# A long-convolution and MLP kernel: the filter spectrum and its exchange in two channel halves, all spectral products on VectorE, the identity made on the chip, and a new order of the pieces

## The chip, the cores and the metric

The kernel runs on one core of one Trainium2 chip. The metric is the time of one execution on the device, in microseconds (us); lower is better. "Span" is what the profile of one execution covers, here about 2 us less than the time. Every ratio of two kernels in this text is the mean time of one kernel's fast runs over that of the other's fast runs of the same rounds on the same chip, with a 95% interval; it is therefore not quite the ratio of the medians that are quoted beside it.

Engines are called PE (TensorE matmul), PEld (its weight load), DVE (VectorE), ACT (ScalarE), POOL (GpSimd) and SP (the engine that issues most DMAs here). PEclk is the TensorE clock that was granted, as a share of full speed. In this kernel PE writes its results to a memory called PSUM, and DVE or ACT copies them from there to SBUF, where the other data on the chip lies; that copy is called an eviction.

## The reference

One block `A` is a causal long convolution by FFT with a gate; one block `B` is an MLP. Each follows a layernorm, and the pair is applied twice.

```python
def _A_ref(q, k, v, shift_k, ssm_k, ssm_D):          # S = 2048, D = 512
    k_shift = sum of 4 shifted copies of k, each times a column of shift_k   # (shortened)
    kv = k_shift * v
    y_f = rfft(pad(kv, 2S)) * rfft(pad(ssm_k, 2S))
    y = irfft(y_f)[:, :S]                            # in bfloat16
    return q * (y + kv * ssm_D)
def _B_ref(x, w1, b1, w2, b2):                       # F = 1376
    return gelu(layernorm(x) @ w1 + b1) @ w2 + b2

x = A_q
x = x + _A_ref(layernorm(x), A_k, A_v, A_shift_k, A_ssm_k, A_ssm_D)
x = x + _B_ref(layernorm(x), ...)
x = x + _A_ref(layernorm(x), ...)                    # the same k, v, filter: y is the same
x = x + _B_ref(layernorm(x), ...)
```

The convolution result does not depend on `x`, so the kernel computes it once. What follows it, eight passes of the MLP over 512 tokens, is the second part of the kernel.

## The kernel before

The transforms are matmuls against tables. The kernel is written as named pieces, each with one engine, and one list gives the order in which they are issued. An engine executes its own pieces in that order, so a piece that waits holds up all later ones on its engine.

How to read the list: `K2S0.P10` is the piece `K2S0` on PE with numbered buffers (PSUM buffer 1, another buffer 0); a name ending in `e` is the eviction of that piece from PSUM; `.A`, `.D`, `.G` and `.S` are ACT, DVE, POOL and the DMA queue. The pieces that matter here, with `c` for a 128-channel chunk (0 to 3):

- `lK`, `lk`, `lv`, `lW`, `lx`: loads. `KTc`: transposes of a loaded filter chunk. `dtc`: adds `ssm_D` to the filter's first time step. `dgc`: four diagonal 128x128 matrices for the shift, made of the identity.
- `KcS`, `KcT`, `K2j`: the stages of the filter's transform. `saj`, `sbj`: DMAs that copy the finished spectrum with its two partition halves exchanged (real against imaginary parts), a quarter at a time.
- `kvc`, `UcS`, `UcT`, `Xcj`: the shifted `k`, times `v`, and its transform. `Tcj`: the product of a piece of that spectrum with the filter's, 16 in all. `Vcj`, `TPc`, `Yc`: the inverse. 
- `s`, `ga`, `gl`, `gp`, `gb`, `h`, `hs`, `LT`: gate and layernorm of the first two MLP passes, and transposes. `ph`: the first matmul of the MLP, with gelu on ACT.

The list in its parts that matter (cut):

```python
ORDER = """
lK2.S dg0.D lK1.S lK3.S ... dg2.D lk3.S lk1.S dg3.D dg1.D dt2.D KT2.P0
...
K0T1.P1 lM.S kT1e.A K3T1.P2 K0T1e.D K27.P0 K24.P3 K3T1e.D K27e.A kv31.P1 K24e.D
K214.P2 kvm31.D K215.P0 K214e.A ... K29.P1 ... K212.P2 ... K28.P1 ... K21.P3 ... K23.P2 ...
... K213.P2 U0S3e.A K211.P3 K25.P1 ...
sb3.S sa3.S K22.P2 ... K20.P1 ... K210.P0 sa0.S sb0.S ... K26.P2
... sa2.S sb2.S U1S2e.D U2S3.P1 U2S0e.A sa1.S sb1.S ...
... X10.P10 ... T10.G0 ... T11.D1 ... T13.G2 ... T00.D0 ... T01.G1 ...
"""
```

The code of the pieces concerned (cut):

```python
nc.scalar.dma_start(sT[:], A_shift_k.rearrange("(ct p) k -> p ct k", p=P))
nc.scalar.dma_start(IDt[:], ident_h.ap().bitcast(BF16))      # the identity comes from HBM
...
dt = plan.add(f"dt{ct}", {"D": 70}, [lK[ct]], lambda it, ct=ct: nc.vector.tensor_tensor(
    Kraw[:, ct, 0:1], Kraw[:, ct, 0:1], Dc[:, ct:ct + 1], ALU.add))
...                                                          # KT waits for dt
for j in range(4):                                           # the exchange, by quarters of all channels
    r = slice(8 * j, 8 * j + 8)
    a = load(f"sa{j}", KSW[0:64, r, :], ZK[64:128, r, :], 2 ** 19, KW[4 * j:4 * j + 4] + ...)
    b = load(f"sb{j}", KSW[64:128, r, :], ZK[0:64, r, :], 2 ** 19, KW[4 * j:4 * j + 4] + ...)
...
def mul(it, px=px, k0=k0, c0=c0):                            # T: 128x2048 elements, by DVE or POOL
    eng = nc.vector if it["eng"] == "D" else nc.gpsimd
    ...
    eng.tensor_tensor(view(Tb[it["slot"]["T"]], [2, 8, CW]), x2, kk, ALU.mult)
```

Of the kernel before, what the change touches and what calls it, by code (L numbers as in the profile page):

```python
# [9 lines left out]
BF16 = mybir.dt.bfloat16  # L10
# [8 lines left out]
lK2.S dg0.D lK1.S lK3.S lH.S lv0.S lK0.S lk2.S lW.S lv1.S lG.S lk0.S dg2.D lk3.S lk1.S dg3.D dg1.D dt2.D KT2.P0  # L19
KT2e.D dt1.D K2S0.P10 KT1.P2 K2S0e.A K2S1.P3 dt3.D KT1e.D KT3.P0 K2S1e.A K2S3.P1 KT3e.D K1S0.P21 K2S3e.A K2S2.P3  # L20
K1S0e.D K1S1.P0 K2S2e.A K1S2.P1 K1S1e.D K1S3.P2 K1S2e.A K2T0.P3 K1S3e.A K3S0.P12 K2T1.P0 dt0.D K3S0e.D K2T0e.A
KT0.P2 K2T1e.D kT2.P1 KT0e.A K3S2.P3 kT2e.D K1T0.P0 K3S2e.A K3S1.P2 K1T0e.D K3S3.P1 K3S1e.A K0S0.P30 K1T1.P0
K0S0e.D K3S3e.A K0S2.P2 K1T1e.D K0S1.P1 K0S2e.A K3T0.P3 K0S1e.A K0S3.P0 kT0.P2 K0S3e.D K3T0e.A kT3.P1 K0T0.P0
kT3e.D kT0e.A kT1.P3 K0T0e.D K0T1.P1 lM.S kT1e.A K3T1.P2 K0T1e.D K27.P0 K24.P3 K3T1e.D K27e.A kv31.P1 K24e.D
K214.P2 kvm31.D K215.P0 K214e.A kv00.P3 K215e.D K29.P1 kvm00.D K212.P2 K29e.A kv10.P0 K212e.D U0S0.P31 kvm10.D
K28.P1 U0S0e.A kv01.P2 K28e.D U1S0.P00 kvm01.D K21.P3 U1S0e.A U1S1.P1 K21e.D K23.P2 U1S1e.A U0S2.P0 K23e.D
U0S1.P3 U0S2e.A kv20.P1 U0S1e.D U0S3.P0 kvm20.D K213.P2 U0S3e.A K211.P3 K25.P1 K213e.D kv11.P0 K25e.A K211e.D
sb3.S sa3.S K22.P2 kvm11.D K20.P1 kv21.P3 K20e.A K22e.D K210.P0 sa0.S sb0.S kvm21.D U1S3.P1 K210e.A K26.P2
U1S3e.D U2S0.P32 K26e.A U1S2.P0 sa2.S sb2.S U1S2e.D U2S3.P1 U2S0e.A sa1.S sb1.S U2S2.P2 U2S1.P3 U2S2e.A U2S3e.D
U1T0.P0 U2S1e.A kv30.P2 U1T0e.D X10.P10 kvm30.D X11.P31 X10e.A U1T1.P0 X11e.A U3S0.P20 T10.G0 U1T1e.D U0T0.P1  # L30
U3S0e.A U3S2.P3 U0T0e.D X13.P02 U3S2e.A U3S1.P2 U3S3.P1 T11.D1 X13e.A U0T1.P3 U3S3e.D X00.P01 U0T1e.A T13.G2
X00e.D X01.P10 X01e.A V10.P31 U3S1e.D U2T0.P0 V10e.A T00.D0 V11.P1 U2T0e.A T01.G1 X03.P21 X02.P32 X03e.D X02e.A
V13.P0 U2T1.P2 T03.D2 V11e.A V00.P32 V13e.A U2T1e.D X21.P11 T02.G0 X20.P00 V00e.D X21e.A V03.P2 X20e.A V01.P3
T21.D2 V03e.A U3T0.P1 T20.D1 X22.P01 V01e.A U3T1.P2 U3T0e.D X22e.A X23.P30 U3T1e.D X12.P12 X23e.A V02.P0 X12e.A
lx.S V20.P20 T22.G0 V02e.A T23.D1 V21.P3 V20e.A T12.D2 X32.P10 V23.P0 X32e.A V21e.D X30.P22 V23e.A V12.P1 T32.G1
X30e.D X33.P31 V12e.A V22.P0 T30.D2 X33e.A TP00.P2 V22e.A X31.P12 TP00e.D TP10.P3 TP20.P0 X31e.D TP10e.A T33.G0
Y00.P2 s00.D TP28.P1 Y00e.A Y10.P3 TP28e.A V30.P20 Y10e.D T31.G2 V30e.A V32.P1 s10.D V33.P3 V32e.A Y28.P2 V33e.A
TP18.P1 Y28e.A TP08.P3 TP18e.A TP20e.D s01.G w2.S w1.S w4.S w3.S V31.P2 s11.G TP08e.D Y20.P0 V31e.A Y18.P1 s02.D
Y20e.A Y08.P3 Y18e.A TP30.P2 ga.D Y08e.A TP34.P0 TP38.P1 s12.A TP30e.D gs.D Y30.P3 Y30e.A TP38e.A gl2.D gl0.D
gp02.G TP34e.A Y38.P2 gp00.G gb02.D Y34.P3 Y38e.A LT02.P1 gb00.D Y34e.A LT02e.A h2.D LT00.P0 LT00e.A h0.D hs2.D  # L40
hs0.D gp12.G gb12.D gp10.G gb10.D
# [78 lines left out]
def kernel(ctx: ExitStack, tc: tile.TileContext, A_q, A_k, A_v, A_shift_k, A_ssm_k, A_ssm_D,  # L120
# [25 lines left out]
    ident_h = nc.inline_tensor(_to_bf16_uint16(np.eye(P, dtype=np.float32)), name="ident128")  # L146
# [20 lines left out]
    ZK = place("ZK", [P, NA, D], 0)  # L167
    ZX = place("ZX", [P, NA, D], 32 * K)
# [12 lines left out]
    Dc = const.tile([P, CT], BF16, name="Dc")  # L181
# [8 lines left out]

    nc.scalar.dma_start(sT[:], A_shift_k.rearrange("(ct p) k -> p ct k", p=P))
    nc.scalar.dma_start(IDt[:], ident_h.ap().bitcast(BF16))
    nc.scalar.dma_start(Ft[:], F_h.ap().bitcast(BF16))
    nc.gpsimd.dma_start(Dc[:], apf(A_ssm_D, 0, [[1, P], [P, CT], [1, 1]]))
# [8 lines left out]
    CW = 128  # L203

# [58 lines left out]
    KSW = place("KSW", [P, NA, D], 64 * K)  # L263
# [3 lines left out]
    V2 = place("V2", [P, NA, D], 0)  # L267
# [22 lines left out]
    with tc.tile_pool(name="ps", bufs=1, space=bass.MemoryType.PSUM) as ps:  # L290
# [20 lines left out]
        def first_stage(name, src, cs, dst, deps):  # L311
# [3 lines left out]
            for q in range(4):  # L315
                def mms(o, q=q):
                    for i in range(4):
                        nc.tensor.matmul(o[:, i, :], src[:, 4 * q + i, cs], Ft[:].rearrange("p x m -> p (x m)"),  # L318
                                         start=True, stop=True)
                hold = {}  # L320

                def zdst(q=q, hold=hold):
                    return view(ZTb[hold["pe"]["slot"]["zt"]], [NT, 2 * P])[:, 4 * q:4 * q + 4, :]
                pe, ev = mm_evac(f"{name}S{q}", 470, deps[q // 2] + [z], mms, [4, 2 * P], zdst,
                                 take=["zt"] if q == 0 else [])
                z = z or pe
                hold["pe"] = z
                ze.append(ev)
            first, out = [], []
            for h in range(2):  # L330
                def mms(o, h=h):
                    for i in range(16):
# [3 lines left out]
                pe, ev = mm_evac(f"{name}T{h}", 980, ze + first, mms, [16, P],  # L336
                                 lambda h=h: dst[:, 16 * h:16 * h + 16, cs], True,
# [15 lines left out]
        KS1, KTR = [], []  # L353
        for ct in range(CT):
            cs = slice(ct * P, ct * P + P)

            dt = plan.add(f"dt{ct}", {"D": 70}, [lK[ct]], lambda it, ct=ct: nc.vector.tensor_tensor(  # L357
                Kraw[:, ct, 0:1], Kraw[:, ct, 0:1], Dc[:, ct:ct + 1], ALU.add))

# [3 lines left out]
            _, e = mm_evac(f"KT{ct}", 950, [dt], mms, [NT, P], lambda cs=cs: Ktok[:, :, cs], True)  # L363
            _, out = first_stage(f"K{ct}", Ktok, cs, ZK, [[e], [e]])
            KTR += list(enumerate(out))
        KW = []
        for j in range(NA // 2):
            def mms(o, j=j):
                for i in range(2):
                    nc.tensor.matmul(o[:, i, :], Wt[:, 2 * j + i, :], ZK[:, 2 * j + i, :], start=True, stop=True)  # L370
            _, ev = mm_evac(f"K2{j}", 440, [lW] + [e for h, e in KTR if h == j // 8], mms, [2, D],
                            lambda j=j: ZK[:, 2 * j:2 * j + 2, :])
            KW.append(ev)
        KX = []
        for j in range(4):
            r = slice(8 * j, 8 * j + 8)
            a = load(f"sa{j}", KSW[0:64, r, :], ZK[64:128, r, :], 2 ** 19, KW[4 * j:4 * j + 4] + [e for _, e in KTR])
            b = load(f"sb{j}", KSW[64:128, r, :], ZK[0:64, r, :], 2 ** 19, KW[4 * j:4 * j + 4] + [e for _, e in KTR])
            KX.append([a, b])


        kTp, kTe, dg = [], [], []
        for ct in range(CT):
            def diag(it, ct=ct):
                for t in range(KS):
                    nc.vector.tensor_scalar(out=DG[:, ct, t, :], in0=IDt[:], scalar1=sF[:, ct, t:t + 1], scalar2=None,
                                            op0=ALU.mult)
            dg.append(plan.add(f"dg{ct}", {"D": 640}, [], diag))
        for q in range(4):
# [4 lines left out]
            pe, ev = mm_evac(f"kT{q}", 950, [lk[q]], mms, [4, CT, P], lambda q=q:  # L394
# [5 lines left out]
        for cc in range(4):  # L400
            cs = slice(cc * CW, cc * CW + CW)
            um = []
            for o2 in range(2):
# [6 lines left out]
                pe = plan.add(f"kv{cc}{o2}", {"P": 1900}, kTe + [dg[cc]],  # L410
# [7 lines left out]
            z, zu = first_stage(f"U{cc}", uv, cs, ZX, [[um[0]], [um[1]]])  # L418
# [6 lines left out]
        TC = {"D": 1220, "G": 4600}  # L425
        PART = [[(0, 8), (8, 16)]] * 3 + [[(0, 4), (4, 8), (8, 16)]]
        for cc in range(4):
# [3 lines left out]
            for j in range(4):  # L431
                k0 = 8 * j

                def mms(o, k0=k0, cs=cs):
                    for i in range(8):
                        nc.tensor.matmul(o[:, i, :], Wt[:, k0 + i, :], ZX[:, k0 + i, cs], start=True, stop=True)  # L436
                hold = {}
                px, xe = mm_evac(f"X{cc}{j}", 480, [ZU[cc][j // 2], lW], mms, [8, CW],
# [3 lines left out]
                def mul(it, px=px, k0=k0, c0=c0):  # L442
                    eng = nc.vector if it["eng"] == "D" else nc.gpsimd
                    kk = at(64 * K + 2 * (k0 * D + c0), [[-32 * K, 2], [D, 8], [1, CW]])
# [3 lines left out]
                tm = plan.add(f"T{cc}{j}", TC, [xe] + KX[j] + KW[4 * j:4 * j + 4], mul, take=["T"],  # L448
# [11 lines left out]
                if INV[cc] == "D":  # L460
                    _, ev = mm_evac(f"V{cc}{j}", 950, [tm, lM], mms, [8, CW],
                                    lambda k0=k0, cs=cs: ZX[:, k0:k0 + 8, cs], free_mm=[(tm, "T")])
                else:
# [4 lines left out]
                    pe, ev = mm_evac(f"V{cc}{j}", 950, [tm, lM, v0], mms, [8, P], vdst, free_mm=[(tm, "T")],  # L468
# [6 lines left out]
            def yout(t0, t9, deps, last):  # L475
                g = Gt if INV[cc] == "D" else GPt

                def mms(o, cs=cs):
                    for i in range(t9 - t0):
                        for x in range(2):  # L480
                            nc.tensor.matmul(o[:, i, :], g[:, x, :], V2[:, 16 * x + t0 + i, cs],
                                             start=x == 0, stop=x == 1)
                _, ev = mm_evac(f"Y{cc}{t0}", 119 * (t9 - t0), deps + [lG, lH] + kvp, mms, [t9 - t0, CW],
# [3 lines left out]
            if INV[cc] == "D":  # L487
                def tr(it, cs=cs):
                    nc.vector.transpose(V2[:, :, cs].bitcast(F32).rearrange("p k c -> p c k"),
                                        ZX[:, :, cs].bitcast(F32).rearrange("p b c -> p c b"))  # L490
# [3 lines left out]
            else:  # L494
                tp = []
                for n, (t0, t9) in enumerate(PART[cc]):
# [8 lines left out]
                    def dst(t0=t0, t9=t9, cs=cs):  # L505
                        return V2[:, :, cs].rearrange("p (x t) c -> p x t c", x=2)[:, :, t0:t9, :]
# [162 lines left out]
```

## Time and profile before

| | before |
|---|---|
| time, median of 3 runs | 306.15 us (305.33 to 308.15) |
| span of the profiled run | 303.5 us |
| first `ph` matmul (the MLP begins) | 139.5 us |

The busy page cuts the span into 40 slices of 7.6 us; a digit is the busy share in tenths, and for PEclk the granted clock in tenths. These are its lines for PE, PEclk and DMA:

```profile
PE   0699999995396599947999999999999999999995
PEclk9999999999589979979999999999999999999999
DMA  6990240599600000640000000000000010010111
```

From the twentieth digit on, PE is full: that is the MLP, which the change leaves alone. Most room is where the digits are low: the first two, the tenth to fourteenth, the eighteenth and nineteenth. Under the 3 of PE stands a clock digit of 5, and after it an 8: PE runs slowly for a while when it has stood still. The Trainium skill, "TensorE: Matmul & The Clock Gate", Part 1, says that an idle PE falls back to half clock; this trace agrees (the clock was 0.50 from 78 to 84 us, after PE had stood still from 72.7).

The waits of PE (columns: engine, what it works on, line, what ended the wait; us in total, times, longest):

```profile
PE p_116 L362 <- DVE arena L357: 9.1, 1, 9.1
PE p_117 L436 <- DVE ZT_88 L220: 7.9, 1, 7.9
PE p_118 L481 <- ACT arena L218: 3.6, 1, 3.6
PE p_116 L459 <- DVE T_95 L447: 3.1, 1, 3.1
```

The same view for DVE has the line that explains the second of them:

```profile
DVE T_95 L447 <- DMA arena<-arena: 7.6, 1, 7.6
```

DVE's product `T11` stands for 7.6 us and waits for the exchange; DVE's later evictions queue behind it, and PE queues behind those. The DMA line of the page shows why it is late: the DMA engines have nothing to do in the seventh slice and are full in the ninth and tenth. The first exchange DMA is issued only at 55.3 us.

The start, by the timeline (columns: start, duration, engine, line, operation, output and inputs, how many; in brackets the idle time before it and what ended it):

```profile
1.25 0.52 ACTq L192 DMA_DIRECT2D IDt<-ident  x1
6.28 2.69 DVE L386 TENSOR_SCALAR DG<-IDt,sF 128x128 bf16<-128x128 bf16 x16 [6.28 <-DMA IDt<-ident]
8.89 0.15 DVE L357 TENSOR_TENSOR arena<-arena,Dc 128x1 bf16<-128x1 bf16 x1
9.10 1.93 PE L362 MATMUL p_116<-IDt,arena 128*128 128x128 bf16 x16 [9.10 <-DVE arena L357]
```

It is one chain: the identity's DMA, 16 diagonal matrices on DVE, the little `dt` add, the first transpose on PE at 9.10 us.

The products, by the timeline of POOL and of DVE:

```profile
86.42 4.08 POOL L447 TENSOR_TENSOR T_95<-xb_91,arena 128x2048 bf16<-128x2048 bf16 x1 [9.82 <-PE p_117 L459]
90.46 5.06 POOL L447 TENSOR_TENSOR T_94<-xb_93,arena 128x2048 bf16<-128x2048 bf16 x1
```

```profile
88.19 3.40 DVE L447 TENSOR_TENSOR T_96<-xb_92,arena 128x2048 bf16<-128x2048 bf16 x1 [0.19 <-PE p_116 L459]
93.94 2.67 DVE L447 TENSOR_TENSOR T_96<-xb_92,arena 128x2048 bf16<-128x2048 bf16 x1
96.53 1.21 DVE L447 TENSOR_TENSOR T_95<-xb_91,arena 128x2048 bf16<-128x2048 bf16 x1
```

The same product takes 1.21 us on DVE when POOL is not busy, and 3.40 or 2.67 us when POOL is. Add start and duration: POOL's product that began at 86.42 ends at 90.50, DVE's slow one at 91.59. The next pair ends at 95.52 and 96.61, and two later pairs at 104.65 and 105.74 and at 111.69 and 112.76. Each time the DVE product ends 1.07 to 1.09 us after POOL's, which is about one undisturbed product, as if DVE's had begun only when POOL was done. It holds the other way too: POOL's longest products, 5.06 and 4.87 us (from 90.46 and from 111.88 us), are the two that began while such a DVE product was still running. The Trainium skill, "SBUF — State Buffer", section "SBUF: two separate sides", describes just this, an exclusive lock on a pair of ports for the whole instruction, which holds back a DVE instruction with two SBUF inputs when a GpSimd instruction reads SBUF; these four pairs agree.

Last, the engines' work by stretch. The boundaries are the first transpose (9.1, the row before is left out), the first `K2`, the first `X`, the end of the last product, and the first `ph`:

```profile
core 0: us, PE busy (x) PEld busy (x) DVE busy (x) ACT busy (x) POOL busy (x), PEclk, DMA share, GB/s
9.10:36.70 27.60, 26.17 (x320) 24.42 (x321) 17.64 (x18) 19.64 (x16) 0.19 (x1) 1.00 0.54 207
36.70:65.80 29.10, 28.11 (x352) 23.13 (x356) 26.20 (x23) 14.99 (x16) 0.00 (x0) 1.00 0.49 138
65.80:122.60 56.80, 42.61 (x634) 41.50 (x632) 42.96 (x45) 35.99 (x34) 35.37 (x11) 0.88 0.27 76
122.60:139.50 16.90, 11.04 (x157) 10.19 (x156) 15.48 (x42) 15.04 (x17) 4.33 (x8) 0.90 0.48 168
139.50:303.50 164.00, 158.98 (x800) 75.66 (x815) 93.38 (x225) 76.68 (x117) 16.62 (x28) 1.00 0.04 14
```

In the product stretch of 56.8 us neither PE nor DVE is busy for more than 43 us. (PEclk says 1.00 in the first row, but the trace has no clock record before 17.4 us: the first 16 transposes took 1.93 us, later ones 1.16.) The product stretch is where most of the room lies; the start adds 9 us, and the MLP's 164 us are fixed.

### The profile page before, as it was taken

What the parts mean: (1) busy time and instruction counts of PE and PEld (TensorE: products, weight loads), DVE (VectorE), ACT (ScalarE), POOL (GpSimd) and SP (SyncE); (2) the same over time, 40 slices, a digit from 0 to 9 for tenths busy, and PEclk for the clock granted to TensorE, in tenths of its full rate; (3) what the DMA queues carried; (4) which work ended last, traced back from release to release, by engine and by line L of the source; (5) the groups of instructions that cost most, each with busy time, mean ns of one, the idle gap of its engine ahead of it and who ended that gap; (6) DMA issues with size and microseconds to landing.
All of it is one profiled execution on the core that took longest, in us unless ns stands there. A gap on an engine that the chain in (4) does not pass through costs nothing.

```text
span 303.5 us, 5479 instructions
## 1 busy us (share of the span) xinstructions
PE 266.9 (88%) x2251; PEld 174.9 (58%) x2272; DVE 198.4 (65%) x366; ACT 163.6 (54%) x198; POOL 59.7 (20%) x58
## 2 busy tenths in 40 slices
PE   0699999995396599947999999999999999999995
PEld 0589988695396599934544444444444454454442
DVE  1378798982669899999987987686875840020231
ACT  1178935576177469988863662633716626337100
POOL 4000000009065678422231001110111100000000
PEclk9999999999589979979999999999999999999999
DMA  6990240599600000640000000000000010010111
GB/s 211 370 411 11 69 209 2 132 219 233 252 2 2 0 2 2 221 153 0 2 1 0 2 0 0 4 0 0 2 0 0 0 54 17 17 39 16 35 54 52
DMA packets 7995, 21.24 MB, mean 70 GB/s; under 512 B 1473, under 2 KB 5282, under 8 KB 6818
## 3 DMA queue, kind: packets, MB, share of 16 engines
q1 hardware_dynamic: 7042, 20.78, 21.1%
q8 instruction: 18, 0.29, 0.4%
q10 hardware_dynamic: 816, 0.10, 0.2%
q0 software_dynamic: 112, 0.00, 0.2%
q14 instruction: 7, 0.06, 0.1%
HBM read 14.59 MB, written 2.10 MB: 55 GB/s over the span
## 4 chain that ended last, share of the span: by engine, by line
PE 65%; DVE 18%; DMA 5%; ACT 4%; issue 3%; POOL 2%; SPq 1%; ACTq 0%; DVEq 0%; POOLq 0%
PE po L615 22%; PE ph L603 19%; DMA arena<-arena 4%; ACT arena L218 2%; DVE arena L220 2%; PE p_116 L335 2%; DVE arena L254 2%; DVE T_95 L447 2%; PE pt L594 2%; DMA IDt<-ident 2%; PE p_116 L459 1%; DVE lst_109 L236 1%; SPq L298 1%; PE p_119 L409 1%; PE p_117 L459 1%
## 5 line engine op out<-in xcount | busy, mean ns | idle before, releaser
L615 PE MATMUL po<-arena 128*128 128x512 bf16 (+1 forms) x338 | 78.9, 379 | 0.9 <-DVE arena L618 0.2
L603 PE MATMUL ph<-arena 128*128 128x512 bf16 (+1 forms) x350 | 77.2, 379 | 1.2 <-ACT arena L218 1.1
L605 ACT ACTIVATE arena<-ph,B_74 128x512 bf16<-128x512 f32 (+1 forms) x88 | 60.4, 687 | 27.1 <-PE ph L603 27.1
L603 PEld LDWEIGHTS <-arena 128*128 128x128 bf16 (+1 forms) x352 | 35.2, 100 | 42.0 <-issue 1.2
L618 DVE TENSOR_TENSOR arena<-po,arena 128x512 bf16<-128x512 f32 x32 | 21.9, 683 | 52.0 <-PE po L615 52.0
L615 PEld LDWEIGHTS <-arena 128*128 128x128 bf16 (+1 forms) x352 | 33.8, 98 | 37.7 <-issue 0.3
L595 ACT ACTIVATE arena<-pt 128x512 bf16<-128x512 bf16 x28 | 15.2, 594 | 38.5 <-PE pt L594 38.2
L409 PEld LDWEIGHTS <-arena 128*128 128x128 bf16 x256 | 14.9, 98 | 1.4
L318 PEld LDWEIGHTS <-arena 128*128 128x128 bf16 x128 | 12.2, 101 | 5.2 <-DVE arena L220 1.6
L447 POOL TENSOR_TENSOR T_94<-xb_91,arena 128x2048 bf16<-128x2048 bf16 x1 | 4.1, 4087 | 56.5 <-ACT xb_92 L218 56.5
L436 PEld LDWEIGHTS <-Wt 128*128 128x128 bf16 x128 | 8.5, 104 | 9.2 <-issue 9.2
L220 DVE COPY arena<-p_116 128x2048 bf16<-128x2048 bf16 x9 | 11.0, 1220 | 4.3 <-PE p_116 L362 3.3
L218 ACT ACTIVATE arena<-p_117 128x1024 bf16<-128x1024 f32 (+2 forms) x8 | 10.8, 1348 | 5.0 <-PE p_117 L370 2.6
L218 ACT ACTIVATE arena<-p_119 128x2048 bf16<-128x2048 bf16 (+2 forms) x8 | 11.6, 1456 | 1.6 <-PE p_119 L503 0.9
L436 PE MATMUL p_117<-arena,Wt 128*128 128x128 bf16 x48 | 4.1, 234 | 9.0 <-DVE ZT_88 L220 7.9
L362 PEld LDWEIGHTS <-arena 128*128 128x128 bf16 x64 | 6.4, 162 | 9.3 <-DVE arena L357 9.1
L362 PE MATMUL p_116<-IDt,arena 128*128 128x128 bf16 x32 | 3.8, 312 | 9.1 <-DVE arena L357 9.1
L236 DVE BATCH_NORM_STATS2 lst_105<-arena 128x6 f32<-128x512 bf16 (+2 forms) x20 | 11.2, 579 | 0.3
L594 PEld LDWEIGHTS <-arena 128*128 128x128 bf16 x112 | 8.0, 97 | 5.8 <-issue 3.1
L245 POOL TENSOR_TENSOR lrs_107<-lrs_107,mhalf 128x4 f32<-128x4 f32 (+1 forms) x5 | 4.6, 923 | 33.6 <-DVE lnm_108 L242 33.6
L218 ACT ACTIVATE ZT_88<-p_117 128x1024 bf16<-128x1024 f32 x5 | 5.1, 1021 | 11.1 <-PE p_117 L318 10.9
L236 DVE BATCH_NORM_STATS2 lst_109<-arena 128x6 f32<-128x512 bf16 x16 | 10.9, 689 | 0.3
(168 smaller groups left out, 458.0 us busy)
## 6 DMA issues: line engine op xcount, KB each, us to landing
arena<-arena SPq DMA_DIRECT2D x8, 512.0 KB, 9.8
arena<-in_A_ssm_k_dram SPq DMA_DIRECT2D x4, 512.0 KB, 6.9
arena<-in_A_v_dram SPq DMA_DIRECT2D x2, 1024.0 KB, 10.4
arena<-in_A_k_dram SPq DMA_DIRECT2D x4, 512.0 KB, 11.5
arena<-tabM SPq DMA_DIRECT2D x1, 2048.0 KB, 8.9
arena<-in_A_q_dram SPq DMA_DIRECT2D x1, 2048.0 KB, 11.4
out_dram<-arena SPq DMA_DIRECT2D x16, 128.0 KB, 1.7
arena<-in_B_w_dram SPq DMA_DIRECT2D x1, 1376.0 KB, 10.8
```

Of the source, the lines that this page charges most:

```text
L218: nc.scalar.activation(dst, src, AF.Copy)
L220: nc.vector.tensor_copy(dst, src)
L236: nc.vector.bn_stats(self.st[:, i, h, :], x_t[:, GT * g + i, c0:c9])
L318: nc.tensor.matmul(o[:, i, :], src[:, 4 * q + i, cs], Ft[:].rearrange("p x m -> p (x m)"), start=True, stop=True)
L409: nc.tensor.matmul(o[:, i, :], w, DG[:, cc, t, :], start=t == 0, stop=t == KS - 1)
L436: nc.tensor.matmul(o[:, i, :], Wt[:, k0 + i, :], ZX[:, k0 + i, cs], start=True, stop=True)
L594: nc.tensor.transpose(pt[:, ct, :], ln[:, i, ct * P:(ct + 1) * P], IDt[:])
L595: nc.scalar.activation(lt[:, :, i * P:(i + 1) * P], pt[:], AF.Copy)
L603: nc.tensor.matmul(ph[0:m, :], W1t[:, ct, ft * P:ft * P + m], lt[:, ct, :], start=ct == 0, stop=ct == CT - 1)
L605: nc.scalar.activation(ht[0:m, ft, :], ph[0:m, :], AF.Gelu_apprx_tanh, bias=B1[0:m, ft:ft + 1])
L615: nc.tensor.matmul(po[:], ht[0:m, ft, i * P:(i + 1) * P], W2t[0:m, ft, :], start=ft == 0, stop=ft == FT - 1)
L618: nc.vector.tensor_tensor(xs, po[:], xs, ALU.add)
```

## The change

It means to take the three waits away. The identity is made on POOL, so nothing waits for its load; the diagonal matrices move to POOL; `dt` is added after the transpose, as a row instead of a column. The spectra are stored in two halves of 256 channels, and the exchange runs half by half, so that the first half can leave before the second is computed. All 16 products run on DVE. And the list has a new order throughout: products are no longer in the same sequence of chunks, and three of the four normalizations `gb` of the layernorm tail go to ACT. The core of the diff (cut):

```diff
-nc.scalar.dma_start(IDt[:], ident_h.ap().bitcast(BF16))
+nc.gpsimd.memset(IDt[:], 1.0)
+nc.gpsimd.affine_select(IDt[:], IDt[:], [[-1, P]], ALU.is_equal, 0.0, base=0, channel_multiplier=1)
+nc.scalar.dma_start(Dc[:], apf(A_ssm_D, 0, [[D, 1], [1, D]]))
...
-            dt = plan.add(f"dt{ct}", {"D": 70}, [lK[ct]], lambda it, ct=ct: nc.vector.tensor_tensor(
-                Kraw[:, ct, 0:1], Kraw[:, ct, 0:1], Dc[:, ct:ct + 1], ALU.add))
+            e = plan.add(f"dt{ct}", {"D": 130}, [e], lambda it, cs=cs: nc.vector.tensor_tensor(
+                Ktok[0:1, 0, cs], Ktok[0:1, 0, cs], Dc[:, cs], ALU.add))        # e: eviction of KT
...
-    ZK = place("ZK", [P, NA, D], 0)
+    ZK = place("ZK", [P, 2, NA, D // 2], 0)          # likewise ZX, KSW, V2
...
-        for j in range(4):
-            r = slice(8 * j, 8 * j + 8)
-            a = load(f"sa{j}", KSW[0:64, r, :], ZK[64:128, r, :], 2 ** 19, KW[4 * j:4 * j + 4] + [e for _, e in KTR])
+        for f in range(2):
+            ...                                       # K2 of half f: 8 pieces of 4 x 256 columns
+            for j in range(2):
+                r = slice(16 * j, 16 * j + 16)
+                KX[f].append([load(f"s{w}{f}{j}", KSW[a:a + 64, f, r, :], ZK[64 - a:128 - a, f, r, :], ...)
+                              for w, a in (("a", 0), ("b", 64))])
...
-                    nc.vector.tensor_scalar(out=DG[:, ct, t, :], in0=IDt[:], ...)
+                    nc.gpsimd.tensor_scalar(out=DG[:, ct, t, :], in0=IDt[:], ...)
...
-        TC = {"D": 1220, "G": 4600}
+        TC = {"D": 1220}                              # and T10.G -> T10.D etc. in the list
...
-hs0.D gp12.G gb12.D gp10.G gb10.D
+LT02e.A hs2.D TP28e.A hs0.D gp12.G Y38e.A Y28.P2 gb12.A gp10.G Y28e.D gb10.A
```

## The prediction

> **What bounds the kernel now.** From 139.5 us (first `ph` matmul) to 303.5 us the MLP keeps PE 90% busy or more (busy tenths): 164 us, untouched by the change. Before it lies the convolution stage, where no engine is full: to 139.5 us (busy time by windows) PE works about 105 us, DVE 106, ACT 88. The gain must come from PE's 34.5 idle us there:
> - 9.1 at the start (waits): PE waits for the `dt` add, behind 16 DG products on DVE (6.28 to 8.97), which wait for the identity's DMA.
> - 7.9 at 73 to 80.6: product T11 waits 7.6 us for the exchange DMAs (chain of waits), PE behind it. The granted clock falls to 0.50; until about 84 us matmuls run slower, some 2.5 us more. The Trainium skill, "TensorE: Matmul & The Clock Gate", Part 1, says that idle PE falls to half clock; the trace agrees.
> - about 8 at 88 to 112, around slow products.
> - about 6 at 129 to 139.5, in the layernorm tail.
>
> **Removed, added, moved.**
> - Identity and DG on GpSimd (DG 3.2 us per four in the change's own plan, done by about 18 us, needed after 30), `dt` behind the transpose. The first transpose waits for its load alone (soonest landing 3.6 us after an issue, here at 0.76), so starts at about 4.7: saves 4.4 us.
> - Exchange by halves: 4.2 MB, about 19 us at the 220 GB/s seen. Half 0 is issued at about 48 us, first needed at 59 (estimates); the wait and the cold clock go.
> - All products on DVE. GpSimd's eight took 4.04 to 5.06 us; four of DVE's eight overlapped them and took 2.67 to 4.31 in place of 1.22. The skill's "GPSIMD Engine Reference", Specifications, says that they share SBUF interfaces; the trace agrees. DVE's eight cost 18.2 us; sixteen at 1.22 cost 19.5.
>
> **Sum.** This trace's durations on the new order, largest engine sum per stretch: first transpose to first K2 21.6 (PE), plus 2 cold, plus 3 waits; to the first exchange 15.2 (PE); to the first X 9.5 (PE); to the last product 39 (DVE; PE 36, ACT 38), plus 12% of bubbles. So the last product ends at 102 to 103; before, at 122.6.
>
> The tail: After the last product ACT carries about 18 us, then TP28's eviction and Y28 precede the first `ph` matmul: about 20 us, against 16.9. And gb12 and gb10, now on ACT, and the 1.28 us table load precede the first gelu, so PE, with three `ph` buffers, stalls about 2 us more.
>
> Span: 103 + 20 + 2 + 164 = 289 us; time about 2 more: **291 us**, range **284 to 299**. Faster by over 2% 0.92, within 2% 0.07, slower 0.01.
>
> **What would show it.** First transpose at 4.5 to 6 us; no DVE wait over 1 us for an exchange; clock 1.00 at 70 to 90 us; every product at 1.2 us; first `ph` matmul at 120 to 126 us, after a PE wait of 1.5 to 3 us on TP28's eviction; early PE wait on gelu of 1 to 3 us.
>
> **What would make it wrong.** More bubbles where PE, DVE and ACT are all about 90% full (each 5% is 2 us); DG over 1.5 us each; `lx` landing late (2 MB took 8.9 us, about 8 us of DVE work covers it); exchange DMAs queuing.

## The result, and the profile after

| | before | after |
|---|---|---|
| time, median of 4 runs each of the same rounds | 306.66 us (305.33 to 308.15) | 285.27 us (284.63 to 285.96) |
| ratio | | 0.930 (0.925 to 0.935) |
| span of the profiled run | 303.5 | 283.2 |

The outputs agreed with the reference. The busy page after (slices of 7.1 us):

```profile
PE   3999999999998973779999999999999999999995
PEclk9999999999999999799999999999999999999999
DMA  7993607994300380000000000000000010110111
```

The hole in the middle is gone, and with it the low clock; one weaker place remains at the fifteenth and sixteenth digit, just before the MLP, with a little clock lost behind it. The waits of PE:

```profile
PE p_117 L363 <- DMA arena<-in_A_ssm_k_dram: 4.9, 1, 4.9
PE p_119 L489 <- ACT arena L223: 2.9, 1, 2.9
PE p_117 L489 <- DVE arena L225: 2.5, 1, 2.5
PE ph L611 <- ACT arena L613: 1.7, 1, 1.7
```

DVE has no wait for the exchange at all any more. The start, by the timeline: the identity is ready at 1.56 us, the first transpose waits for its load alone, and the diagonal matrices run on POOL beside the transposes:

```profile
1.27 0.29 POOL L191 TENSOR_SCALAR_AFFINE_SELECT IDt<-IDt 128x128 bf16<-128x128 bf16 x1
4.90 1.92 PE L363 MATMUL p_117<-IDt,arena 128*128 128x128 bf16 x16 [4.90 <-DMA arena<-in_A_ssm_k_dram]
10.04 9.30 POOL L394 TENSOR_SCALAR DG<-IDt,sF 128x128 bf16<-128x128 bf16 x16
```

The products, from the view of their line (columns: operation, how many, least/median/greatest ns, first and last start; one of its lines):

```profile
L455 DVE TENSOR_TENSOR T_95<-xb_92,arena x5: 1214/1215/1220, 56.0 to 94.0; 128x2048 bf16<-128x2048 bf16 x5
```

Every one of the 16 products takes 1.21 to 1.23 us, 19.5 us together. And the same stretches as before, by windows (columns as above):

```profile
4.90:28.40 23.50, 23.49 (x305) 22.51 (x306) 19.39 (x20) 14.55 (x14) 9.64 (x18) 1.00 0.81 293
28.40:53.50 25.10, 24.95 (x359) 23.74 (x358) 18.32 (x16) 15.02 (x17) 0.00 (x0) 1.00 0.54 155
53.50:95.20 41.70, 39.83 (x627) 38.20 (x626) 40.27 (x51) 37.98 (x40) 5.33 (x6) 1.00 0.40 106
95.20:116.60 21.40, 13.76 (x208) 13.00 (x207) 20.62 (x60) 19.14 (x20) 4.32 (x8) 0.95 0.41 133
116.60:283.20 166.60, 160.78 (x819) 75.97 (x816) 88.46 (x204) 79.08 (x121) 14.15 (x24) 0.99 0.04 13
```

Set against before (row by row, and the start from the first marks), the start gives 4.2 us (9.1 to 4.9), the filter's first stages 4.1 (27.6 to 23.5), the stretch to the first `X` 4.0, and the product stretch 15.1 (56.8 to 41.7): 27.4 us in all. The tail takes 4.5 us of it back (16.9 to 21.4) and the MLP 2.6 (164.0 to 166.6). That leaves 20.3 us, which is the difference of the two spans. The marks do not bound the same work, though: the new order puts 16 transposes (`K0T1`) behind the first `K2`, and one `kv` piece and six `UcS` pieces more than before behind the first `X`. So part of what the early rows gain is work that was moved to later rows.

In the product stretch PE, DVE and ACT are now all between 91 and 97% busy: there is little left to win by moving work between them. The tail is different. The timeline of its end (some lines left out):

```profile
112.13 1.02 ACT L223 ACTIVATE arena<-p_120 128x1024 bf16<-128x1024 bf16 x1 [0.43 <-PE p_120 L559]
113.05 1.87 ACT L223 ACTIVATE arena<-p_118 128x2048 bf16<-128x2048 bf16 x1
114.98 1.87 PE L489 MATMUL p_119<-arena,GPt 128*128 128x128 bf16 x16 [2.88 <-ACT arena L223]
116.64 3.44 PE L611 MATMUL ph<-arena 128*128 128x512 bf16 x12
121.80 3.40 PE L611 MATMUL ph<-arena 128*128 128x512 bf16 x15 [1.72 <-ACT arena L613]
```

The first line is the eviction of the last `LT`, the second that of `TP28`. `Y28`, PE's last piece ahead of the MLP, waits 2.88 us for that second eviction, which ACT reaches only after the `LT`s. Five microseconds after the MLP has begun, PE stands still once more for 1.72 us, for the first gelu. Both were in the prediction; the experiments also ask whether they can be taken away.

### The profile page after: what moved, and what is told of

It is laid out like the page before. It is cut to its first block, busy times and chain, and to the rows that moved or that the text cites. A ratio compares the mean times of both kernels' runs of the same rounds, so it can differ in the third digit from the quotient of the medians.

```text
span 283.2 us, 5560 instructions
## 1 busy us (share of the span) xinstructions
PE 262.8 (93%) x2304; PEld 173.4 (61%) x2304; DVE 187.1 (66%) x346; ACT 167.1 (59%) x210; POOL 36.1 (13%) x67
## 4 chain that ended last, share of the span: by engine, by line
PE 79%; DVE 13%; ACT 4%; issue 2%; DMA 1%; POOL 0%; ACTq 0%; DVEq 0%
PE ph L611 26%; PE po L623 26%; PE p_119 L417 3%; PE pt L602 2%; PE p_118 L340 2%; DVE lst_106 L241 2%; DVE T_96 L455 2%; PE p_119 L340 1%; DMA arena<-in_A_ssm_k_dram 1%; PE p_117 L340 1%; PE p_120 L323 1%; ACT arena L603 1%; PE p_118 L417 1%; PE p_117 L323 1%; PE p_118 L323 1%
## 5 line engine op out<-in xcount | busy, mean ns | idle before, releaser
L623 PE MATMUL po<-arena 128*128 128x512 bf16 (+1 forms) x352 | 80.7, 379 | 0.0
L603 ACT ACTIVATE arena<-pt 128x512 bf16<-128x512 bf16 x28 | 15.2, 594 | 38.4 <-PE pt L602 38.2
L417 PEld LDWEIGHTS <-arena 128*128 128x128 bf16 x256 | 15.0, 98 | 0.2
L223 ACT ACTIVATE arena<-p_118 128x1024 bf16<-128x1024 f32 (+1 forms) x8 | 10.0, 1247 | 6.5 <-PE p_118 L377 4.7
L323 PEld LDWEIGHTS <-arena 128*128 128x128 bf16 x128 | 11.9, 99 | 1.9 <-issue 0.4
L225 DVE COPY arena<-p_117 128x2048 bf16<-128x2048 bf16 x6 | 7.3, 1220 | 8.0 <-PE p_117 L363 6.9
L489 PEld LDWEIGHTS <-GPt 128*128 128x128 bf16 x128 | 8.3, 104 | 6.4 <-issue 3.7
L602 PEld LDWEIGHTS <-arena 128*128 128x128 bf16 x112 | 8.0, 97 | 6.1 <-issue 3.6
L225 DVE COPY arena<-p_119 128x2048 bf16<-128x2048 bf16 (+1 forms) x9 | 10.4, 1159 | 1.0 <-PE p_119 L511 0.6
L241 DVE BATCH_NORM_STATS2 lst_110<-arena 128x6 f32<-128x512 bf16 x16 | 10.8, 687 | 0.3
L223 ACT ACTIVATE arena<-p_119 128x1024 bf16<-128x1024 f32 (+3 forms) x8 | 9.5, 1190 | 2.4 <-PE p_119 L377 1.8
L602 PE MATMUL pt<-IDt,arena 128*128 128x128 bf16 x112 | 9.6, 218 | 0.5
L241 DVE BATCH_NORM_STATS2 lst_102<-arena 128x6 f32<-128x512 bf16 x16 | 9.9, 680 | 0.1
L241 DVE BATCH_NORM_STATS2 lst_98<-arena 128x6 f32<-128x512 bf16 x16 | 9.9, 679 | 0.1
L394 POOL TENSOR_SCALAR DG<-IDt,sF 128x128 bf16<-128x128 bf16 x16 | 9.3, 598 | 0.1
## 6 DMA issues: line engine op xcount, KB each, us to landing
out_dram<-arena SPq DMA_DIRECT2D x16, 128.0 KB, 1.7
```

The lines of the kernel that those rows point to most:

```text
L223: nc.scalar.activation(dst, src, AF.Copy)
L225: nc.vector.tensor_copy(dst, src)
L241: nc.vector.bn_stats(self.st[:, i, h, :], x_t[:, GT * g + i, c0:c9])
L323: nc.tensor.matmul(o[:, i, :], src[:, 4 * q + i, cs], Ft[:].rearrange("p x m -> p (x m)"), start=True, stop=True)
L417: nc.tensor.matmul(o[:, i, :], w, DG[:, cc, t, :], start=t == 0, stop=t == KS - 1)
L602: nc.tensor.transpose(pt[:, ct, :], ln[:, i, ct * P:(ct + 1) * P], IDt[:])
```

## The experiments

Twelve kernels ran, all with correct outputs. One run of the kernel before fell at 334.92 us and is left out as not fast. The theory was that the gain has three separate causes: the start (the identity's load and what follows it), the late exchange, and POOL's products, and that the rest is the new order. The main rivals: that the identity alone does it, that the exchange must be halved by channels to remove the stall, and that POOL's products cost nothing but their own length.

| run | built on | what it is | median us | ratio to before (95%) |
|---|---|---|---|---|
| e1_ident | before | identity on the chip only | 306.02 | 0.998 (0.991 to 1.005) |
| e2_head | before | whole start | 301.76 | 0.985 (0.979 to 0.991) |
| e3_xorder | before | `K2` and exchange reordered only | 297.42 | 0.970 (0.963 to 0.976) |
| e4_prodD | before | products on DVE only | 302.99 | 0.989 (0.983 to 0.995) |
| e5_three | before | e2, e3 and e4 together | 290.31 | 0.947 (0.943 to 0.951) |
| e6_dummy | after | six idle POOL products added | 293.13 | 0.956 (0.952 to 0.960) |
| e7_gbD | after | two normalizations back on DVE | 284.88 | 0.929 (0.926 to 0.933) |
| e8_tail | after | tail reordered | 281.38 | 0.919 (0.915 to 0.923) |
| e9_control | after | unchanged | 285.65 | 0.932 (0.929 to 0.935) |
| e10_load | after | order of loads: `k` by its use, two small ones last | 284.65 | 0.928 (0.926 to 0.931) |
| e11_tail2 | after | e8, one PSUM buffer changed | 280.22 | 0.916 (0.912 to 0.920) |
| e12_all | after | e10 and e11 | 279.52 | 0.911 (0.908 to 0.914) |

e1 to e4 shared one chip and the runs of the kernel before, e5 to e8 another, e9 to e12 a third. Where a gain in us is worked out below, it is (1 - ratio) times 306.2 us; for e1 to e4 the interval makes it uncertain by about 2 us either way. By the record's verdicts, which ask for 2%, e1 and e4 are "same" and e2 is "unclear"; that e2 and e4 gained something rests on their intervals, which leave out 1.

A warning about single profiles. The times of the 28 fast runs of the kernel before go with the mean granted clock: 305.3 to 306.0 us at 0.970 to 0.972, 306.0 to 306.6 at 0.964, 307.4 to 308.4 at 0.958 to 0.959. And two profiles of the changed kernel, the one above and e9's, have their first `ph` at 116.6 and 118.1 us. A difference of 1 to 2 us between two marks can be no more than where PE's half-clock stretches fell.

### e1_ident: the identity alone

```diff
-nc.scalar.dma_start(IDt[:], ident_h.ap().bitcast(BF16))
+nc.gpsimd.memset(IDt[:], 1.0)
+nc.gpsimd.affine_select(IDt[:], IDt[:], [[-1, P]], ALU.is_equal, 0.0, base=0, channel_multiplier=1)
```

> The kernel before, with one part alone: the identity is made on GpSimd instead of loaded; DG stays on VectorE and the dt add stays in front of the transpose. Theory (three serial causes hide one behind the other: identity, 16 DG products, dt with its own Dc load that landed at about 7.9 us in the profile before): the first transpose starts at 7.9 to 8.7 us instead of 9.1 and the time falls by 0.3 to 1.3 us. Rival (the identity's DMA is the cause of the 9.1 us): first transpose at about 5 us, time down by about 4 us.

The first transpose moved only from 9.10 to 8.52 us and the time not measurably (ratio 0.998, interval around 1). With the identity's load away, the diagonal matrices still wait for the shift weights (to 4.96 us), and the `dt` add, on DVE behind them, then waits for the load of `ssm_D`:

```profile
8.30 0.16 DVE L357 TENSOR_TENSOR arena<-arena,Dc 128x1 bf16<-128x1 bf16 x1 [0.65 <-DMA Dc<-in_A_ssm_D_dram]
```

The identity's load ended the wait in the profile of before, but it was not the only thing there to wait for.

### e2_head: the whole start

```diff
 (e1, and)
-    Dc = const.tile([P, CT], BF16, name="Dc")        # loaded by POOL's queue
+    Dc = const.tile([1, D], BF16, name="Dc")         # loaded by ACT's queue, before sT
-            dt = plan.add(... Kraw[:, ct, 0:1], Kraw[:, ct, 0:1], Dc[:, ct:ct + 1] ...)   # before KT
+            e = plan.add(... Ktok[0:1, 0, cs], Ktok[0:1, 0, cs], Dc[:, cs] ...)           # after KT's eviction
-dg0.D ... dg2.D ... dg3.D dg1.D dt2.D KT2.P0 KT2e.D dt1.D
+dg0.G ... dg2.G ... dg3.G dg1.G KT2.P0 KT2e.D dt2.D
```

> The kernel before with the whole start of the change: identity and DG on GpSimd, dt after the transpose on one partition, small loads in the order of the changed kernel; the rest of the order, the exchange and the products as before. Theory: first transpose at 4.9 us, and the 4.2 us carry through to the end, because everything behind it, the exchange included, is released by the work and not by the clock on the wall: time down by 3.5 to 5 us. Rival (the exchange stall is set by the transfers and swallows it): time down by less than 2 us and DVE's wait for the exchange grows from 7.6 to 10 us or more.

The first transpose starts at 4.77 us, the first `K2` at 33.0 (36.7 before), the first `ph` at 135.5 (139.5), and the ratio 0.985 is a gain of 4.6 us. So the start's gain passes through to the end; the stall for the exchange is still there at 7.5 us and only moves with it.

### e3_xorder: the order of `K2` and exchange alone

The pieces stay in quarters of all channels. Only the list is edited: the four pieces of a quarter follow one another and its two DMAs are issued right after, and the quarters go in the order 0, 1, 3, 2.

```diff
-K27 K24 K214 K215 K29 K212 K28 K21 K23 K213 K211 K25   sb3 sa3   K22 K20 K210   sa0 sb0   K26   sa2 sb2 sa1 sb1
+K20 K21 K22 K23 sa0 sb0   K24 K25 K26 K27 sa1 sb1   K212 K213 K214 K215 sa3 sb3   K28 K29 K210 K211 sa2 sb2
 (other pieces between them unchanged)
```

> The kernel before, with only the order of the exchange changed: the sixteen K2 pieces are renamed so that they finish in groups of four and each group's two transfers are issued as soon as its four evictions are in; no halving by channels, same transfers of 512 KB, products and start as before. Theory (the order of the K2 pieces made the exchange late; halving by channels is one way to mend it, not the only one): no wait of DVE over 1 us for a transfer, granted clock 1.00 from 70 to 90 us, time down by 6 to 11 us. Rival (without channel halves the exchange can't be ready in time): a wait of over 4 us remains and the time falls by less than 4 us.

The first exchange DMA is issued at 42.3 us where it was 55.3. DVE has no wait for a DMA in this stretch any more, and PE's clock stays full where it had fallen to half; the window says so (columns as above):

```profile
70.00:80.00 10.00, 8.56 (x135) 8.09 (x133) 9.45 (x8) 8.98 (x9) 9.08 (x3) 1.00 0.59 212
```

The ratio 0.970 is a gain of 9.3 us (7.4 to 11.3), about the 7.9 us of the wait. That the rest is the slow clock after it is not shown: in this profile another stretch at half clock, from 123.4 to 133.7 us, reaches into the MLP. The rival that halving by channels is needed to remove the stall is ruled out. This was the largest single cause.

### e4_prodD: the products alone

```diff
-T10.G0 T13.G2 T01.G1 T02.G0 T22.G0 T32.G1 T33.G0 T31.G2
+T10.D0 T13.D2 T01.D1 T02.D0 T22.D0 T32.D1 T33.D0 T31.D2
```

> The kernel before with all sixteen products on VectorE, nothing else changed, each at the same place of the order. Theory (a product on GpSimd holds the VectorE product that meets it until it ends, so GpSimd's help costs VectorE about as much as it saves, and GpSimd's 4 to 5 us are latency for the V stage): every product 1.2 us, DVE's busy sum for products 19.5 against 18.2 us, and the stretch from the end of the exchange stall (80.6 us) to the first ph matmul, 58.8 us before, falls by 2 to 6 us. Rival (VectorE was the scarce engine and GpSimd relieved it): that stretch and the time grow by 2 to 8 us.

All products take 1.2 us, and from 80.6 us, where the stall of before ends, to the first `ph` there are 53.7 us where there were 58.8. The ratio 0.989 is a gain of 3.4 us; the stall for the exchange remains. The first `ph` came 5.2 us earlier (134.3), so some 2 us were lost again behind it. The windows show where: from 134.3 to 140.0 us the clock was 0.63 and PE finished 16 matmuls of `ph` in 5.67 us, while before it finished 25 in the first 5.5 us of the MLP, at full clock. The half-clock stretch lasts from 128.3 to 138.5 us here; before, the one in the tail ended at 136.8, ahead of the MLP. Why it lasts longer is not shown: PE was idle about as long in both tails (6.2 and 5.9 us).

### e5_three: the three together

The edit is e2, e3 and e4.

> The kernel before with the three parts tried alone put together: the new start, the earlier exchange (K2 pieces renamed, no halving by channels), all products on VectorE; otherwise the order before. Theory (three separate stretches of the chain, so their gains add): 4.6 + 9.3 + 3.4 us, measured one by one, give a time of about 289 us (287 to 291), and what is left to the changed kernel's 285 is the new order's own part, in the stretch from the first transpose to the first K2 (27.6 us before, 23.5 after). Rival (the parts overlap, for instance the earlier exchange only uncovers the products): 292 us or more. Second rival (halving by channels is what the change lives on): the same, with a wait of VectorE on a transfer.

The gains of the three add up to 4.6 + 9.3 + 3.4 = 17.3 us; together they bring 16.3 us. They add up within the noise, so the three causes explain about three quarters of the change's 21.4 us. The remaining 5.1 us belong to what e5 lacks, the storage in channel halves and the new order. By the marks, e5 needs 27.6 us from the first transpose to the first `K2` and the change 23.5; to the first `X`, 28.6 and 25.1. But part of that is moved work: ahead of its first `X` e5 issues 640 matmuls apart from those of `K2`, the change 600; it does the rest later. From the first transpose to the first `ph`, PE was busy for 105.0 of 117.4 us in e5 and for 102.0 of 111.7 in the change: 3.0 us less work time and 2.7 us less idle time. The clock had a share in this that was not separated: it was at half from 114.3 to 127.9 us in e5, and only from 114.6 to 118.0 in the change. e5's windows of the product stretch and the tail (columns as above):

```profile
60.90:102.30 41.40, 37.28 (x600) 35.74 (x598) 39.89 (x43) 33.69 (x31) 3.12 (x4) 1.00 0.19 62
102.30:122.10 19.80, 14.06 (x193) 12.99 (x191) 18.62 (x53) 17.25 (x19) 3.29 (x7) 0.80 0.43 144
```

The tail of 19.8 us is a finding too. Before, it was 16.9; with the old tail order unchanged, 2.9 us of the 4.5 us that the change gives back are there already. In part this is the mark: the last product now ends earlier among the other pieces, so that 193 matmuls are left behind it, against 157 before. In part it may be the clock, 0.80 against 0.90. The other 1.6 us came with the new order (e9's profile of the changed kernel would say 2.3). And here too the MLP starts cold: from 122.1 to 128.0 us the clock was 0.51.

### e6_dummy: POOL's products as bystanders

Six products whose output nothing uses are put on POOL at the place of the first real ones. They read SBUF and write a free place. If POOL costs DVE nothing, the time stays.

```diff
+        for i in range(6):
+            plan.add(f"zz{i}", {"G": 4100}, [ZU[0][0]], lambda it: nc.gpsimd.tensor_tensor(
+                <lna0 as 16 x 128>, chunk(ZX, 0)[:, 0:16, :], chunk(ZX, 0)[:, 0:16, :], ALU.mult))
-U0T0e.D K214.P0
+U0T0e.D zz0.G zz1.G zz2.G zz3.G zz4.G zz5.G K214.P0
```

> The changed kernel with six extra products of the same shape on GpSimd during the product stage (about 54 to 80 us): they read finished data and write a free buffer, nothing waits for them. Result stays right. Theory (exclusive use: a VectorE product that meets a running GpSimd product stands until that one ends): VectorE products that start inside such a GpSimd instruction end 1.0 to 1.2 us after its end, the longest takes 3 to 5.3 us in place of 1.22, evictions from PSUM keep 1.2 us, and the time grows by 4 to 15 us. Rival (GpSimd products cost only by their own latency, when something waits for them): all VectorE products stay at 1.2 us and the time stays within 1 us.

The time rises by 7.9 us (0.956 - 0.930, times 306.2) although nothing waits for these six. Two groups of DVE's work between 48 and 80 us (columns: line, engine, operation, how many; busy us, mean ns; idle before):

```profile
L457 DVE TENSOR_TENSOR T<-xb,arena 128x2048 bf16<-128x2048 bf16 x5 | 13.9, 2809 | 0.0
L224 DVE COPY arena<-p 128x2048 bf16<-128x2048 bf16 x6 | 7.2, 1220 | 1.7 <-PE p L339 1.1 <-ACT xb L222 0.4
```

The five products, with two inputs in SBUF, take 2.81 us on average, the longest 4.62, in place of 1.22. The evictions, whose input lies in PSUM, keep their 1.22 us; so do the two `kvm` products that DVE ran meanwhile (1.22 and 1.21 us), a `tensor_tensor` as well but with one input in PSUM. So the cost falls on the one kind of instruction and not on the other, as the Trainium skill, "SBUF — State Buffer", section "SBUF: two separate sides", has it. In narrow windows the timelines of POOL and DVE show the single products (two pairs of three):

```profile
59.05 4.46 POOL L432 TENSOR_TENSOR arena<-arena 128x2048 bf16<-128x2048 bf16 x1
59.97 4.62 DVE L457 TENSOR_TENSOR T<-xb,arena 128x2048 bf16<-128x2048 bf16 x1
71.81 3.60 POOL L432 TENSOR_TENSOR arena<-arena 128x2048 bf16<-128x2048 bf16 x1
72.41 4.09 DVE L457 TENSOR_TENSOR T<-xb,arena 128x2048 bf16<-128x2048 bf16 x1
```

DVE's end 1.08 and 1.09 us after POOL's (the third pair: 2.92 us on DVE, 1.07 after), as in the trace of before. Only these three of the five met POOL. The five cost 13.9 - 5 x 1.22 = 7.8 us more, and the time went up by 7.9, so hardly anything hid it (the equality is not exact: this profile also has a wait of 1.1 us for a load, of which more below).

### e7_gbD: the stall at the first gelu

The change had put two normalizations, `gb12` and `gb10`, on ACT ahead of the first gelu. Here they go back to DVE.

```diff
-Y38e.A Y28.P2 gb12.A gp10.G Y28e.D gb10.A
+Y38e.A Y28.P2 gb12.D gp10.G Y28e.D gb10.D
```

> The changed kernel with gb12 and gb10, the last layernorm pieces of the second token group, back on VectorE in place of ScalarE. Theory (they and the table load stand before the first gelu, so PE waits for a ph buffer): the PE wait on gelu of 1.7 us goes, first gelu at about 118 in place of 121 us, time down by 1.2 to 2.2 us. Rival (the wait comes back elsewhere, for VectorE is as full as ScalarE there): time within 0.5 us.

The stall is gone from the profile, and from the first `ph` to the end it is 164.8 us, not 166.6. The time is 284.88 us against 285.27, or against 285.65 of the control below, on other chips: less than the run-to-run spread. The profiled run lost elsewhere what it had gained here; its first `ph` came at 118.4, not 116.6. It has a wait for a load of `k` that the profile of the change does not have:

```profile
PE p L400 <- DMA arena<-in_A_k_dram: 1.4, 1, 1.4
```

That wait is hardly the reason, though: the control (e9), which has none, has its first `ph` at 118.1 us, a stall at the gelu of only 0.9 us, and the clock at half at nearly the same two places as e7. So the mechanism is confirmed and its worth to the time is not: on that, this run missed what was expected.

### e8_tail: the tail reordered

`TP28`'s eviction goes ahead of the `LT`s' on ACT, three normalizations (`gb`) go back to DVE, `Y28`'s eviction goes to ACT, and the PSUM buffers of the last pieces are dealt out anew.

```diff
-gp00.G Y34.P0 Y34e.D gp02.G gb00.A h2.D Y38.P0 gb02.D Y18e.A LT00.P2 h0.D LT00e.A LT02.P3 LT02e.A hs2.D TP28e.A
-  hs0.D gp12.G Y38e.A Y28.P2 gb12.A gp10.G Y28e.D gb10.A
+gp00.G Y34.P0 gb00.D Y18e.A gp02.G Y38.P2 TP28e.A LT00.P3 Y34e.D gb02.D LT00e.A LT02.P1 LT02e.A Y28.P0 h2.D h0.D
+  Y38e.A hs2.D hs0.D gp12.G Y28e.A gb12.D gp10.G gb10.D
```

> The changed kernel with the order of the last stretch mended (from gl0 on): TP28's and Y18's evictions go before the LT ones, gb00 and gb02 on VectorE before the h pieces, Y38 into a buffer that is free at once, Y28 after LT02, gb12 and gb10 on VectorE. No work added or taken. Theory (in the changed kernel the first ph matmul waits for TP28's eviction behind LT02's, 2.9 us, and for Y34's, 2.5 us): first ph matmul at 112 to 114 in place of 116.6 us, the stall on gelu under 0.7 us, time down by 3.5 to 6 us. Rival (ScalarE and VectorE are full there, so any order ends alike): first ph matmul within 1 us of 116.6, time down by the 1.7 us of the gelu stall at most.

281.38 us, 3.5 us less than e7 on the same chip. The direction was right, the size not quite: the first `ph` came at 115.7 us, where 112 to 114 was expected. Part of it is again a wait for `k`, 1.6 us. The other part is an oversight:

```profile
PE ph L610 <- ACT arena L222: 2.2, 1, 2.2
```

`Y28` had been given PSUM buffer 0, which is the one that the MLP's first `ph` takes over, so `ph` had to wait for `Y28`'s eviction.

### e9_control, e10_load: is it the load of `k`?

Three of the experiments built on the change (e6, e7, e8) showed a wait of 1.1 to 1.6 us for a load of `k`, and the change's own profile did not. Two small tables are loaded ahead of the large pieces; e10 puts them last and the quarters of `k` in the order of their use, and e9 is the change itself on the same chip as e10.

```diff
-lK1.S dg3.G lK2.S lK3.S lG.S lH.S lK0.S lk1.S lk0.S lk3.S lv1.S lW.S lv0.S lk2.S
+lK1.S dg3.G lK2.S lK3.S lK0.S lk0.S lk3.S lk1.S lv1.S lW.S lv0.S lk2.S lG.S lH.S
```

> The changed kernel itself, unaltered, as control on the chip that runs the next three. Why: the profiles of three of its variants showed a PE wait of 1.1 to 1.6 us for a load of k at about 13 us, which the first profile of the changed kernel did not. If that wait comes and goes with the run or the chip, the control may show it, and its time stays at 284.5 to 286.5 us; the variant with gb12 and gb10 on VectorE, which lost the 1.7 us stall and still measured 284.9, is then explained by the load. Rival: the control has no such wait and still measures 285; then that variant's gain went elsewhere.

> The changed kernel with only the order of loads mended: the quarters of k in the order of their use (0, 3, 1, 2 in place of 1, 0, 3, 2) and the two small tables that are first read at about 80 us behind all the others. Theory (kT0, the first user, waits for the second quarter in the queue, on the edge): no PE wait for k over 0.3 us in the profile, time down by 0.5 to 2 us against the control. Rival (PE is full from 5 to 28 us and the loads are early enough): within 0.5 us of the control.

The control has no such wait and 285.65 us, as the change has. e10 has 284.65 us, 1.0 us less (0.928 over 0.932 is 0.996). The order of the loads is worth that little. Why only e6, e7 and e8 waited stays open: they shared one chip, but the changed kernel itself did not run on it.

### e11_tail2 and e12_all

e11 is e8 with `Y28` in PSUM buffer 3 and its eviction on DVE; e12 adds e10's order of loads.

```diff
-LT02.P1 LT02e.A Y28.P0 h2.D h0.D Y38e.A hs2.D hs0.D gp12.G Y28e.A gb12.D gp10.G gb10.D
+LT02.P1 LT02e.A Y28.P3 h2.D h0.D Y38e.A hs2.D hs0.D gp12.G Y28e.D gb12.D gp10.G gb10.D
```

> The mended tail once more, with one thing put right: in the run with the mended tail the first ph matmul waited 2.2 us for the eviction of Y28, the last one on ScalarE, since Y28 lay in the PSUM buffer that ph takes over first. Here Y28 lies in another buffer and its eviction goes to VectorE between the layernorm pieces. Theory: first ph matmul waits for LT02's eviction alone; time down by another 1 to 2.5 us against the first mended tail, 279 to 280.5 us. Rival (the later start of gb10 on VectorE, or a stall on gelu, takes it back): within 0.5 us of 281.4.

> The mended tail (second form) and the mended load order together on the changed kernel. If their gains are in separate stretches of the chain they add: 277.5 to 280 us, 5 to 7.5 us under the control. Rival: the earlier start of the stretch only meets ScalarE and VectorE, both full at 80 to 112 us, and the sum falls short by over 1 us.

e11 takes 280.22 us and e12 279.52, 5.4 and 6.1 us less than the control beside them. The timeline of e12 shows `Y28` and the first `ph` back to back, and no stall at the gelu over 0.2 us (PE alone):

```profile
111.50 1.05 PE L488 MATMUL p<-arena,GPt 128*128 128x128 bf16 x16 [0.31 <-ACT arena L222]
112.41 2.75 PE L610 MATMUL ph<-arena 128*128 128x512 bf16 x12
```

`Y28` waits 0.31 us, not 2.88, and `ph` begins at 112.4 us, not 116.6. In e11, last product to first `ph` is about 17.1 us, almost the 16.9 of before: what the change had given back in the tail was a matter of order and buffers. The clock is part of that gain: in the profiles of e8, e11 and e12 it stays at 1.00 up to the last microseconds, while the control's is at half from 109.4 to 112.8 and from 116.2 to 119.7 us. e12 is faster than both kernels, by 8.9% and 2.2%.

## Why the prediction was right or wrong

It said 291 us, in a range of 284 to 299; the change took 285.27. The range held and so did "faster by over 2%", but the estimate was 5.7 us too slow. In the table, the span is meant.

| mark (us) | before | predicted | after |
|---|---|---|---|
| first transpose | 9.1 | 4.7 | 4.9 |
| first `K2` | 36.7 | 31.3 | 28.4 |
| end of the last product | 122.6 | 102 to 103 | 95.2 |
| first `ph` | 139.5 | 123 (120 to 126) | 116.6 |
| end of the span | 303.5 | 289 | 283.2 |

What held:

- The start. The first transpose at 4.9 us was inside the 4.5 to 6 that were named, and e1 and e2 show that it took the whole chain, not the identity alone. The diagonal matrices cost POOL 0.60 us each, below the 1.5 us that would have hurt.
- The exchange. No DVE wait for it, and no clock digit below 9 until the tail begins at 95 us. Its first half left at 43.5 us (said: about 48), and the first product began at 56.0 (said: 59). e3 shows it to be worth 9.3 us. But the prediction let the reader think that halves were the means; e3 reached it by order alone. What halving itself is worth was not separated from the new order.
- The products. All at 1.2 us, and their total of 19.5 us was exact. e4 and e6 show the contention from both sides. The prediction rested on the skill's "GPSIMD Engine Reference", Specifications, which says that GpSimd's SBUF interfaces are shared with VectorE; the traces agree.
- The tail. The wait on `TP28`'s eviction (2.88 us, said 1.5 to 3) and the stall at gelu (1.72, said 1 to 3) came as named. The stretch was 21.4 us and not 20. Some of this is luck of the profile: the control's, of the same kernel, has 3.20 and 0.9 us for the two and 22.1 for the stretch.

The prediction's starting point was a little off: it put PE's idle time ahead of the MLP at 34.5 us, where the windows give 31.6 (139.5 - 107.9). What failed in its reasoning is one step, the sum for the time up to the last product. In the prediction's words: "first transpose to first K2 21.6 (PE), plus 2 cold, plus 3 waits", and "plus 12% of bubbles. So the last product ends at 102 to 103". It ended at 95.2. The errors of that sum:

- The terms as written do not give 102 to 103. They are 4.7 + 21.6 + 2 + 3 + 15.2 + 9.5 + 1.12 x 39 = 99.7. About 3.3 us (to the 103 that the next sum used) were padding that no term stands for.
- "3 waits" did not occur. The stretch took 23.5 us, against 26.6, and PE was busy for 23.49 of them. e5, in the old order (with 16 transposes more in the stretch), took 27.6 us, with 2 us of PE idle.
- "12% of bubbles" was too much: 41.7 us and not 43.7. The busiest engine, DVE, had 40.27 us of work in it, so that bubbles were 3.6% of it.
- In the other direction, the start was 0.2 and the stretch from `K2` to `X` 0.4 us longer than said.

3.3 + 3.1 + 2.0 - 0.2 - 0.4 = 7.8 us, which is 103 less 95.2. The tail was then 1.4 us longer than estimated and the rest 0.6, so 5.8 of it stood at the end. The first `ph` at 116.6 us was therefore outside the 120 to 126 that were named. The mechanisms were right; the sizes of waits and bubbles, for which the prediction names no source, were too large for an order that had been made anew to avoid them.

What stays open: how the 5.1 us between e5 and the change divide between storage in halves, new order and granted clock; what the two normalizations are worth alone (e7); and why some profiles waited for `k`.

## What to carry to other kernels

Work moved to a second engine is only free if the two do not lock each other out: look for an instruction whose duration depends on who else runs, and test it with a bystander that nothing waits for. What made the transfer late here was the order of the pieces that feed it, so try issuing these in the order in which the transfer needs them before restructuring the data. Look at the granted clock before reading a difference of 1 or 2 us off one profile each. When the stages ahead get faster, look at the tail again: the evictions on the path go first, and the buffer that the next stage takes over must be the first to come free; and in an estimate every microsecond of padding should belong to a named term.

## What the Trainium skill lacked or had wrong

- "GPSIMD Engine Reference", section 4.1 Engine selection, gives GpSimd as about 2 times slower than VectorE for elementwise instructions with two inputs and roughly at line rate with one. It has no figure for bf16. Here the undisturbed bf16 product of 128x2048 elements took 4.04 to 4.09 us on GpSimd and 1.21 to 1.23 us on VectorE, 3.3 times. With one tensor input and a scalar per partition at 128x128, 16 took 9.30 us against 2.69 us, 3.5 times; how much of that is a fixed cost of each instruction the runs do not separate.
- No page says what the lock costs on the critical path. Here three held-up products (2.92, 4.62 and 4.09 us in place of 1.22) added 7.8 us of DVE time, and the kernel's time rose by 7.9 us (e6_dummy).
